# Activation-beacon attention and a soft MoE on one core: first loads, beacon requests, a weight piece and the next pair's first score bank are moved

## The chip, the cores and the metric

The kernel runs on one core of a Trainium2 chip. The metric is device time in microseconds: before the change 202.38 us, the median of three runs (201.41 to 203.35). The profile is of one further execution.

## The reference

Inputs are float32: q, k, v of 8 batches x 8 heads x 576 tokens x 64, beacon_k and beacon_v of 16 positions per head, phi (512 x 32), and eight experts' w1 (512 x 1024) and w2 (1024 x 512).

```python
k_all, v_all = concat([beacon_k, k], 2), concat([beacon_v, v], 2)
scores = q @ k_all.T / sqrt(64)           # causal among tokens, beacons always seen
a = softmax(scores); x = (a @ v_all)      # -> 4608 tokens x 512
logits = x @ phi                          # 32 slots, 4 for each of 8 experts
slot_in = softmax(logits, over tokens).T @ x
slot_out[e] = relu(slot_in[e] @ w1[e]) @ w2[e]
out = softmax(logits, over slots) @ slot_out
```

So all tokens have to pass attention before any expert can work, and all experts before any output row exists.

## The kernel before

**Work.** Two heads make a pair; there are 32 pairs n, four (g = 0 to 3) in each of 8 batches b. A pair's transposed scores (keys on partitions) go through four PSUM banks; ScalarE exponentiates each bank to float16 (`scores`, L522), POOL zeroes the masked triangle (`select`, L508), TensorE multiplies by v with a column of ones (`attend`), VectorE divides (`normalize`, three instructions, the last one L552), and TensorE turns x for the logits (`x_transposes`). For each half batch, q and k are turned by TensorE and copied out by VectorE (`transposes`, L486 and L498); half m's turning of k comes in one pair and that of q in the next. `logits` makes the slot scores of a batch and exponentiates them into dT, repeated four times; `dispatch` sums x by slot over the batch; `combine_T` turns dT into eT for the output. In the loop these are done a batch or two late, between pairs.

**v.** It is loaded as vstag, four consecutive tokens on a partition, with the 16 beacons on partitions 0 to 3; `cast_v` makes float16 of it on POOL, and `perm_v` puts the rows in order with 16 selecting products into four accumulators, which ScalarE and VectorE copy to vh. The last 80 tokens come apart (`load_vr`).

**Order.** Every engine executes in the order in which the code names its instructions; an instruction waits for its data and for the slot of the tile that it writes. Slots: q and k staging four each, vstag two, score accumulators two (two banks each), the attend accumulator one, the small PSUM tiles (tag tr) two, and x, bkf and their like two (tag x). All loads but two of the first are issued by SP; POOL issues the weight pieces of 512 KB in float16, cast from float32 on the way, 32 of them (`load_weights`, L449 and L456), the last of them into staging slots of q, k and v as these come free.

**Start and end.** Before the loop stand the first loads, constants, `fill` (products without a use, which keep TensorE busy), the turning of the beacon keys through bkh, PSUM and bkA to kT, and pairs 0 and 1. After it stand the last pair's rest, the experts (`first` L823, `turn`, `second` L838), the scaling of the slot outputs (L860), and the output in 13 requests (L920).

Of the kernel before, what the change touches and what calls it, by code (L numbers as in the profile page):

```python
# [9 lines left out]
FP = mybir.dt.float32  # L10
# [258 lines left out]
def kernel(  # L269
# [38 lines left out]
    phih = const.tile([P, NDC, NSL], F16, name="phih")  # L308
    bkA = const.tile([P, Nb, B * H], BF, name="bkA")

# [44 lines left out]
    def load_v(b):  # L355

        t = st["v", b] = stv.tile([P, H, 4, D], FP, name="vstag", tag="v", bufs=2)
        st["r", b] = stv.tile([P, H, D], FP, name="vrem", tag="r", bufs=2)
        if b:
            lo = (b * H * S - Nb) * D
            nc.sync.dma_start(
                out=t[:, :, :, :].rearrange("p h t d -> p h (t d)"),
                in_=v.rearrange("b h s d -> (b h s d)")[lo:lo + H * S * D].rearrange(
                    "(h e) -> h e", h=H)[:, 0:4 * P * D].rearrange("h (p e) -> p h e", p=P))
        else:
            for p0, p1 in ((4, 116), (116, 128)):  # L370
                nc.sync.dma_start(
                    out=t[p0:p1, :, :, :].rearrange("p h t d -> p h (t d)"),
                    in_=v[b, :, 4 * p0 - Nb:4 * p1 - Nb, :].rearrange(
                        "h (p t) d -> p h (t d)", t=4))

    def load_vr(b):
        nc.sync.dma_start(out=st["r", b][0:80, :, :],
                          in_=v[b, :, 496:576, :].rearrange("h p d -> p h d"))

    def load_bv(b):  # L380
        nc.sync.dma_start(out=st["v", b][0:4, :, :, :].rearrange("p h t d -> p h (t d)"),
                          in_=beacon_v[b].rearrange("h (p t) d -> p h (t d)", t=4))

    def cast_v(b, c):

        if c == 0:
            st["c", b] = work.tile([P, 4, H, D], F16, name="vc", tag="vc", bufs=1)
        if c < 2:
            for hs in (slice(4 * c, 4 * c + 2), slice(4 * c + 2, 4 * c + 4)):
                nc.gpsimd.tensor_copy(  # L390
                    out=st["c", b][:, :, hs, :].rearrange("p t h d -> p h t d"),
                    in_=st["v", b][:, hs, :, :])
        else:
            nc.gpsimd.tensor_copy(out=vhs[b % 2][0:80, 4, :, 0:D], in_=st["r", b][0:80, :, :])

    def perm_v(b):

        ps = ps_sc.tile([P, 2, 512], FP, name="vps", tag="sc")
        pt = [ps_tr.tile([P, 512], FP, name="vpt", tag="tr") for _ in range(2)]
        outs = [ps[:, 0, :], ps[:, 1, :], pt[0][:, :], pt[1][:, :]]  # L400
        vc = st["c", b]
        for t in range(4):
            for c in range(4):
                nc.tensor.matmul(outs[c], sel[32 * c:32 * c + 32, t, :],  # L404
                                 vc[32 * c:32 * c + 32, t, :, :].rearrange("p h d -> p (h d)"),
                                 start=(t == 0), stop=(t == 3))
        nc.scalar.activation(vhs[b % 2][:, 0:2, :, 0:D],  # L407
                             ps[:, :, :].rearrange("p c (h d) -> p c h d", d=D), AF.Copy)
        for i in range(2):
            nc.vector.tensor_copy(out=vhs[b % 2][:, 2 + i, :, 0:D],  # L410
                                  in_=pt[i][:, :].rearrange("p (h d) -> p h d", d=D))
# [49 lines left out]

    def beacon_keys(m):
        for hh in range(2):
            c0, c1 = (H * (m // 2) + head(2 * m + u, hh) for u in range(2))
            nc.gpsimd.tensor_copy(  # L465
                out=kTs[m % 2][64 * hh:64 * hh + 64, :, 0:Nb],
                in_=bkA[64 * hh:64 * hh + 64, :, c0:c1 + 1:c1 - c0].rearrange("p n u -> p u n"))

    def transposes(m, which):
# [6 lines left out]
        else:  # L476
            if m:
                beacon_keys(m)
            dst = kTs[m % 2][:, :, Nb:Nb + S]
        for j0, j1 in ((0, 5), (5, NJ)):  # L480
            tp = ps_tr.tile([P, j1 - j0, P], BF, name="trps", tag="tr")
            for j in range(j0, j1):
# [92 lines left out]
    def logits(b, t0=0, t1=NDC):  # L575
# [10 lines left out]
        if t1 < NDC:  # L586
            return
        if t0 == 0:
            nc.scalar.activation(dTs[b][:, :, :, :],
                                 lp[:, :, :].unsqueeze(2).broadcast_to([P, NC5, 4, NSL]), AF.Exp)  # L590
        else:
            nc.scalar.activation(dTs[b][:, :, 0, :], lp[:, :, :], AF.Exp)
            nc.vector.tensor_copy(
                out=dTs[b][:, :, 1:4, :],
                in_=dTs[b][:, :, 0:1, :].broadcast_to([P, NC5, 3, NSL]))

# [76 lines left out]
    with tc.manual_schedule(engines={ET.PE, ET.DVE, ET.Activation, ET.Pool, ET.SP}):  # L673
        load_qk(0, 0, first=True)
        bkf = work.tile([P, Nb, D], FP, name="bkf", tag="x")
        nc.sync.dma_start(out=bkf[0:B * H, :, :].rearrange("p n d -> p (n d)"),
                          in_=beacon_k.rearrange("b h n d -> (b h) (n d)"))
        load_v(0)
        load_bv(0)
        load_vr(0)  # L680
        load_qk(0, 1)
        load_v(1)
        load_qk(1, 0)
        load_bv(1)
        load_vr(1)
        load_qk(1, 1)
        phif = work.tile([P, NDC, NSL], FP, name="phif", tag="phif", bufs=1)
# [4 lines left out]
        make_identity(nc, idb)  # L692
        make_identity(nc, idh)
        for t in kTs:
            nc.gpsimd.memset(t[:, :, Nb + S:640], 0.0)
# [6 lines left out]
        nc.gpsimd.memset(xT[:, :, S:640], 0.0)  # L702
        nc.gpsimd.memset(sel[:, :, :], 0.0)


        fill(10, False)
        transposes(0, 0)
        fill(2, False)
        transposes(0, 1)
        bkh = work.tile([P, Nb, D], BF, name="bkh", tag="vc", bufs=1)  # L710
        hi = bkf[0:B * H, :, :].bitcast(BF)[:, :, 1::2]
        nc.scalar.activation(bkh[0:B * H, 8:Nb, :], hi[:, 8:Nb, :], AF.Copy)
        nc.vector.tensor_copy(out=bkh[0:B * H, 0:8, :], in_=hi[:, 0:8, :])
        bkp = ps_tr.tile([P, Nb, B * H], BF, name="bkps", tag="tr")
        for i in range(Nb):
            for hh in range(2):
                nc.tensor.transpose(bkp[64 * hh:64 * hh + 64, i, :], bkh[0:B * H, i, :],
                                    idb[0:B * H, 0:B * H])
        nc.vector.tensor_copy(out=bkA[:, :, :], in_=bkp[:, :, :])  # L719
        beacon_keys(0)  # L720
        fill(5, False)
        for c in range(4):
            for t in range(4):
                nc.vector.tensor_copy(
                    out=sel[32 * c:32 * c + 32, t, :].rearrange(
                        "p (m t) -> p m t", t=4)[:, :, t],
                    in_=idh[32 * c:32 * c + 32, 32 * c:32 * c + 32])


        scores(0, 0, False)  # L730
        scores(0, 1, False)
        for c in range(2):
            cast_v(0, c)
        for bank in range(2):
            fill(3, False)
            scores(0, 2 + bank, False)
        for bank in range(4):
            select(0, bank)
        cast_v(0, 2)
        for bank in range(3):  # L740
            fill(3, False)
            scores(1, bank)
        transposes(1, 0)
        perm_v(0)
        scores(1, 3)
        transposes(1, 1)
        attend(0, 0)
        attend(0, 1)
        normalize(0)
        load_v(2)  # L750
        load_qk(2, 0)

        for n in range(2, NPAIR):
            b, g = divmod(n, NG)
            scores(n, 0)
            scores(n, 1)
            if n // 2 + 1 < 2 * B:
                transposes(n // 2 + 1, n % 2)
            attend(n - 1, 0)
            scores(n, 2)  # L760
            if n >= 3:
                x_transposes(n - 3)
            attend(n - 1, 1)
            if n >= 7 and g == 3:
                combine_T(b - 1)
            normalize(n - 1)
            scores(n, 3)
            if n == NPAIR - 1:
                x_transposes(n - 2)
            if b and g == 2:  # L770
                logits(b - 1)
            if n >= 8 and g == 0:
                dispatch(b - 2)
            if b + 1 < B and g:
                parts = ((0,), (1,), (2,))[g - 1] if b else ((0,), (1, 2))[g - 2]
                for c in parts:
                    cast_v(b + 1, c)
                if g == 3:
                    perm_v(b + 1)
            if b + 2 < B:  # L780
# [3 lines left out]
                if g == 2:  # L784
                    load_bv(b + 2)
                    load_vr(b + 2)
                    load_qk(b + 2, 1)
            if n == 5:
                nc.vector.tensor_copy(out=phih[:, :, :], in_=phif[:, :, :])
            load_weights((0, 1, 1, 1)[g] if b < 6 else 2)  # L790
        siz = work.tile([P, NDC, E * (NSL + SPE)], F16, name="siz", tag="qT")
# [11 lines left out]
        dispatch(B - 2)  # L803
        fill(2)
        x_transposes(n - 1)
# [154 lines left out]
```

## Time and profile before

| what | value |
|---|---|
| median of three runs | 202.38 us |
| profiled execution, its own time | 200.63 us |
| its span, first to last instruction | 198.9 us |
| granted TensorE clock, mean | 0.956 |
| TensorE busy (82%) | 162.4 us |
| ScalarE busy (67%) | 134.0 us |
| VectorE busy (67%) | 132.4 us |
| POOL busy (58%) | 114.8 us |
| moved by DMA | 55.90 MB |
| SP's queue (q1), share of 16 engines' span | 56.0% |
| POOL's queue (q0, weights), the same | 42.3% |
| first exp of pair 0; pair 4; pair 28 | 12.26; 34.66; 137.68 us |
| last weight request issued | 154.4 us |
| first output request | 170.66 us |

The page gives busy time per engine over the whole span, and a row of 40 slices shows where in the span it lies. The DMA row is the mean busy share of 16 engines. The stretches give the same for any window, with the number of instructions in brackets, then the granted clock, the DMA share and the bytes moved per time. Bytes of the weight pieces are counted after the cast, so 214 GB/s in a stretch of weights alone stands for twice that read. In the timeline a bracket gives the idle time of the engine ahead of an instruction and what ended it.

### The profile page before, as it was taken

The numbers are of one execution on the slowest core, as the hardware profiler recorded it, in microseconds if no ns is written. First come the engines' busy times: TensorE is split into PE (matmuls) and PEld (weight loads), VectorE is DVE, ScalarE is ACT, GpSimd is POOL, SyncE is SP. The second block draws the span as 40 slices with busy tenths as digits, with TensorE's granted clock in tenths as the row PEclk, the third lists the DMA queues.
The fourth block names the chain that finished last, engine by engine and source line by source line (L and its number), as shares of the span: only waits on it lengthen the run. The fifth ranks groups of instructions, "written<-read, shape, count | busy, mean of one in ns | idle before, by whom it ended". The sixth has DMA issues, their size and how long they took to land.

```text
span 198.9 us, 7368 instructions
## 1 busy us (share of the span) xinstructions
PE 162.4 (82%) x3122; PEld 107.9 (54%) x3122; DVE 132.4 (67%) x279; ACT 134.0 (67%) x172; POOL 114.8 (58%) x264
## 2 busy tenths in 40 slices
PE   6798893889898898988989898898978999875200
PEld 2443561667586576756757665675856844542000
DVE  0352684678888888888789778788855532898300
ACT  2356694688888889888888788888787140783200
POOL 6049087359659847955965786799776400890000
PEclk9999999699999999999999999999999999997855
DMA  6999999999999999999999999999999995599991
GB/s 203 258 240 367 283 357 326 264 377 316 280 242 379 279 258 326 319 258 292 381 249 270 363 305 269 257 229 211 216 211 214 214 213 95 211 410 415 409 403 69
DMA packets 29845, 55.90 MB, mean 281 GB/s; under 512 B 7244, under 2 KB 15660, under 8 KB 29804
## 3 DMA queue, kind: packets, MB, share of 16 engines
q1 hardware_dynamic: 24764, 37.98, 56.0%
q0 software_dynamic: 4752, 16.78, 42.3%
q10 hardware_dynamic: 288, 0.59, 1.0%
q8 instruction: 26, 0.43, 0.8%
q14 instruction: 15, 0.12, 0.2%
HBM read 62.69 MB, written 9.44 MB: 363 GB/s over the span
## 4 chain that ended last, share of the span: by engine, by line


## 5 line engine op out<-in xcount | busy, mean ns | idle before, releaser
L522 ACT ACTIVATE expT<-sc 128x992 f16<-128x992 f32 (+3 forms) x128 | 104.8, 867 | 20.3 <-PE sc L517 19.7
L508 POOL TENSOR_SCALAR_AFFINE_SELECT expT<-expT 128x224 f16<-128x224 f16 (+3 forms) x128 | 55.1, 441 | 39.6 <-ACT expT L522 38.7
L517 PE MATMUL sc<-qT,kT 64*128 64x80 bf16 (+4 forms) x576 | 43.7, 246 | 11.2 <-ACT expT L522 5.4
L538 PE MATMUL av<-vh,expT 128*128 128x65 f16 (+1 forms) x960 | 40.3, 195 | 0.2 <-DVE x L552 0.2
L538 PEld LDWEIGHTS <-expT 128*128 128x128 f16 (+1 forms) x960 | 33.6, 98 | 4.3 <-POOL expT L508 0.8
L498 DVE COPY kT<-trps 128x640 bf16<-128x640 bf16 (+1 forms) x31 | 22.7, 773 | 19.6 <-PE trps L486 19.1
L517 PEld LDWEIGHTS <-kT 64*128 64x128 bf16 x576 | 17.1, 95 | 28.2 <-issue 22.4
L498 DVE COPY qT<-trps 128x640 bf16<-128x640 bf16 (+1 forms) x30 | 22.0, 773 | 8.4 <-PE trps L486 6.6
L552 DVE TENSOR_TENSOR x<-av,r 128x640 f16<-128x640 f32 x32 | 26.4, 824 | 1.1
L390 POOL CAST vc<-vstag 128x512 f16<-128x512 f32 x32 | 18.7, 614 | 1.6 <-ACT expT L522 1.6
L571 DVE COPY xT<-xtps 128x576 f16<-128x576 f16 x31 | 14.1, 456 | 6.0 <-PE xtps L564 5.8
L914 ACT ACTIVATE osb<-fps,rc 128x512 f32<-128x512 f32 (+1 forms) x18 | 11.2, 675 | 10.2 <-PE fps L909 9.5
L564 PE MATMUL xtps<-idh,x 128*128 128x128 f16 (+2 forms) x160 | 14.3, 217 | 0.4 <-issue 0.2
L916 DVE TENSOR_SCALAR osb<-fps,rc 128x512 f32<-128x512 f32 (+1 forms) x19 | 12.8, 727 | 1.3 <-PE fps L909 1.2
L658 PE MATMUL fill<-eT,onesh 128*128 128x512 f16 x36 | 11.6, 451 | 1.7 <-POOL onesh L691 1.5
L407 ACT ACTIVATE vh<-vps 128x1024 f16<-128x1024 f32 x8 | 8.2, 1027 | 6.6 <-PE vpt L404 6.6
L410 DVE CAST vh<-vpt 128x512 f16<-128x512 f32 x16 | 10.3, 684 | 3.6 <-PE vpt L404 3.6
L564 PEld LDWEIGHTS <-x 128*128 128x128 f16 (+2 forms) x160 | 9.2, 98 | 6.0 <-issue 5.5
L909 PE MATMUL fps<-so,eT 128*128 128x512 f16 (+1 forms) x37 | 11.2, 431 | 1.2 <-DVE so L860 0.8
L465 POOL COPY kT<-bkA 64x32 bf16<-64x32 bf16 x32 | 7.4, 232 | 7.9 <-DVE bkA L719 7.0
L486 PE MATMUL trps<-idb,kstag 128*64 128x128 bf16 x270 | 11.7, 234 | 0.1
L486 PE MATMUL trps<-idb,qstag 128*64 128x128 bf16 x270 | 10.9, 222 | 0.7 <-DVE vh L410 0.4
(98 smaller groups left out, 187.6 us busy)
## 6 DMA issues: line engine op xcount, KB each, us to landing
kstag<-in_k_dram SPq DMA_DIRECT2D x15, 576.0 KB, 10.0
qstag<-in_q_dram SPq DMA_DIRECT2D x15, 576.0 KB, 13.6
out_dram<-osb SPq DMA_DIRECT2D x11, 768.0 KB, 7.2
vstag<-in_v_dram SPq DMA_DIRECT2D x7, 1024.0 KB, 14.8
w1h<-in_moe_w_dram POOLq DMA_DIRECT2D x10, 512.0 KB, 8.6
w2h<-in_moe_w_dram POOLq DMA_DIRECT2D x10, 512.0 KB, 8.4
wt<-in_moe_w_dram POOLq DMA_DIRECT2D x7, 512.0 KB, 12.2
wv<-in_moe_w_dram POOLq DMA_DIRECT2D x4, 512.0 KB, 11.6
```

The costliest lines, as they stand in the source:

```text
L390: nc.gpsimd.tensor_copy(out=st["c", b][:, :, hs, :].rearrange("p t h d -> p h t d"), in_=st["v", b][:, hs, :, :])
L486: nc.tensor.transpose(tp[lo:hi, j - j0, :], t[:, hh, j, :].bitcast(BF)[:, 1::2], idb[:, :])
L498: nc.vector.tensor_copy(out=do, in_=ti)
L508: nc.gpsimd.affine_select(out=ap, in_=ap, compare_op=AL.is_ge, fill=0.0, base=cbase, pattern=pat, channel_multiplier=-1)
L517: nc.tensor.matmul(sc[:, hh, col:col + qw], kTs[n // 2 % 2][po:po + D, n % 2, c * P:(c + 1) * P], qTs[n // 2][po:po + D, n % 2, q0:q0 + qw ...
L522: nc.scalar.activation(ex[:, :, base:base + w], sc[:, :, 0:w], AF.Exp, scale=scale)
L538: nc.tensor.matmul(av[:, i, :], exps[n % 2][0:KW[c], hh, o:o + P], vhs[b % 2][0:KW[c], c, h, :], start=(c == 0), stop=(c == i))
L552: nc.vector.tensor_tensor(out=xs[b][:, :, head(n, 0):head(n, 1) + 1:head(n, 1) - head(n, 0), :].rearrange("p i h d -> p h i d"), in0=av[:, ...
L564: nc.tensor.transpose(tp[:, QLO[i]:QLO[i] + QW[i]], xs[b][0:QW[i], i, 2 * t:2 * t + 2, :].rearrange("p h d -> p (h d)"), idh[0:QW[i], 0:QW ...
L571: nc.vector.tensor_copy(out=xT[:, t, 0:S], in_=tp[:, :])
L658: nc.tensor.matmul(ps[:, :], onesh[:, :], eT[:, 0:512], start=True, stop=True)
L916: nc.vector.tensor_scalar(out=ou, in0=f[:, 0:hw], scalar1=rc[:, bb, j:j + 1], scalar2=None, op0=AL.mult)
```

## The change

Loads. v of batch 0 comes as one request over 128 partitions for heads 1 to 7 and two requests (60 and 64 partitions) for head 0, whose first four partitions POOL zeroes. `load_bv` is gone: beacon_v of batch 0 comes as 16 partitions x 8 heads and that of all batches as one request of 128 partitions. beacon_k comes as 128 partitions x 2 KB in place of 64 x 4 KB. `load_qk(1, 0)` stands ahead of `load_v(1)`.

v. The selecting matrix has zeros for the beacons' rows, and `perm_v` adds them by one product from bvh. For batch 0 it accumulates in the attend banks, and two of its casts are VectorE's; batch 1's casts stand a pair earlier.

Beacon keys. One copy of bkf by VectorE, 16 products of 128 x 128, and kT written from PSUM by VectorE for half 0; bkA is copied after it.

Loop. `scores(n + 1, 0)` stands at the end of pair n; banks 2 and 3 stand ahead of the two halves of `attend`. `combine_T` moves to g = 0 and `dispatch` to g = 1 of the batch after the next, each behind the bank and behind `normalize`. `logits` exponentiates one copy on ScalarE and VectorE repeats it. One weight piece is issued ahead of the loop, one less in batch 5.

```diff
     def load_v(b):
-        if b:
...
-        else:
-            for p0, p1 in ((4, 116), (116, 128)):
...
+        h0 = 0 if b else 1
+        lo = ((b * H + h0) * S - Nb) * D
+        nc.sync.dma_start(
+            out=t[:, h0:H, :, :].rearrange("p h t d -> p h (t d)"),
...
+        if b == 0:
+            nc.gpsimd.memset(t[0:4, 0, :, :], 0.0)
+            for p0, p1 in ((4, 64), (64, 128)):
                 nc.sync.dma_start(
+                    out=t[p0:p1, 0, :, :].rearrange("p t d -> p (t d)"),
+                    in_=v[b, 0, 4 * p0 - Nb:4 * p1 - Nb, :].rearrange("(p t) d -> p (t d)", t=4))
...
-    def load_bv(b):
...
     def cast_v(b, c):
-                nc.gpsimd.tensor_copy(
+                (nc.vector if c == 1 and b == 0 else nc.gpsimd).tensor_copy(
...
     def perm_v(b):
-        ps = ps_sc.tile([P, 2, 512], FP, name="vps", tag="sc")
+        pool, tag = (ps_sc, "sc") if b else (ps_av, "av")
+        ps = pool.tile([P, 2, 512], FP, name="vps", tag=tag)
...
+        rows(0, 0)
+        lhsT, rhs = (idh[:, b::B], bvh) if b else (idh[0:Nb, 0:Nb], bvh[0:Nb])
+        nc.tensor.matmul(outs[0][0:Nb, :], lhsT, rhs[:, :, :].rearrange("p h d -> p (h d)"),
+                         start=False, stop=False)
...
     def logits(b, t0=0, t1=NDC):
-        if t0 == 0:
-            nc.scalar.activation(dTs[b][:, :, :, :],
-                                 lp[:, :, :].unsqueeze(2).broadcast_to([P, NC5, 4, NSL]), AF.Exp)
-        else:
...
+        nc.scalar.activation(dTs[b][:, :, 0, :], lp[:, :, :], AF.Exp)
+        nc.vector.tensor_copy(
+            out=dTs[b][:, :, 1:4, :],
+            in_=dTs[b][:, :, 0:1, :].broadcast_to([P, NC5, 3, NSL]))
...
         load_v(0)
-        load_bv(0)
+        bv0 = work.tile([P, H, D], FP, name="bv0", tag="x")
+        nc.sync.dma_start(out=bv0[0:Nb, :, :], in_=beacon_v[0].rearrange("h n d -> n h d"))
         load_vr(0)
         load_qk(0, 1)
+        load_qk(1, 0)
         load_v(1)
-        load_qk(1, 0)
-        load_bv(1)
         load_vr(1)
+        bvf = work.tile([P, H, D], FP, name="bvf", tag="x")
+        nc.sync.dma_start(out=bvf[:, :, :], in_=beacon_v.rearrange("b h n d -> n b h d"))
         load_qk(1, 1)
...
         transposes(0, 0)
-        fill(2, False)
+        bkh = work.tile([P, Nb // 2, D], BF, name="bkh", tag="vc", bufs=1)
+        nc.vector.tensor_copy(out=bkh[:, :, :], in_=bkf[:, :, :].bitcast(BF)[:, :, 1::2])
         transposes(0, 1)
...
+        beacon_keys(0, bkp[:, :, :].rearrange("p n (c a) -> p n c a", a=2), nc.vector)
+        nc.vector.tensor_copy(out=bkA[:, :, :, :].rearrange("p n c a -> p n (c a)"),
+                              in_=bkp[:, :, :])
+        fill(3)
...
+        scores(1, 0)
+        perm_v(0)
+        scores(1, 1)
         transposes(1, 0)
-        perm_v(0)
+        scores(1, 2)
+        attend(0, 0)
+        transposes(1, 1)
         scores(1, 3)
-        transposes(1, 1)
-        attend(0, 0)
         attend(0, 1)
         normalize(0)
         load_v(2)
         load_qk(2, 0)
+        load_weights(1)
+        scores(2, 0)
         for n in range(2, NPAIR):
             b, g = divmod(n, NG)
-            scores(n, 0)
             scores(n, 1)
             if n // 2 + 1 < 2 * B:
                 transposes(n // 2 + 1, n % 2)
+            scores(n, 2)
             attend(n - 1, 0)
-            scores(n, 2)
             if n >= 3:
                 x_transposes(n - 3)
+            scores(n, 3)
             attend(n - 1, 1)
-            if n >= 7 and g == 3:
-                combine_T(b - 1)
             normalize(n - 1)
-            scores(n, 3)
             if n == NPAIR - 1:
                 x_transposes(n - 2)
+            else:
+                scores(n + 1, 0)
+            if b > 1 and g == 0:
+                combine_T(b - 2)
+            if b > 1 and g == 1:
+                dispatch(b - 2)
             if b and g == 2:
                 logits(b - 1)
-            if n >= 8 and g == 0:
-                dispatch(b - 2)
...
-                    load_bv(b + 2)
                     load_vr(b + 2)
...
-            load_weights((0, 1, 1, 1)[g] if b < 6 else 2)
+            load_weights((0, 1, int(b < 5), 1)[g] if b < 6 else 2)
...
         dispatch(B - 2)
-        fill(2)
+        combine_T(B - 2)
         x_transposes(n - 1)
```

## The prediction

> **What bounds the kernel now.** The page's slices first: is there an engine without gaps?
>
> ```profile
> PE   6798893889898898988989898898978999875200
> ...
> DMA  6999999999999999999999999999999995599991
> ```
>
> No compute engine fills its slices, but the 16 DMA engines stand at 9 from the second slice to the 33rd, and again while the output leaves. A share of 9 doesn't yet say that useful bytes move, so next the stretches (the last two columns are the DMA share and GB/s):
>
> ```profile
> 6.00:8.00 2.00, 1.94 (x22) 1.16 (x24) 0.82 (x1) 0.51 (x1) 0.00 (x0) 1.00 1.05 202
> 8.00:10.00 2.00, 1.04 (x36) 0.87 (x36) 1.15 (x2) 1.43 (x3) 0.00 (x0) 1.00 1.12 262
> 10.00:12.00 2.00, 2.00 (x30) 0.93 (x26) 1.51 (x9) 0.00 (x0) 0.50 (x2) 1.00 1.29 155
> 12.00:14.00 2.00, 1.87 (x14) 0.72 (x11) 1.02 (x10) 1.74 (x3) 0.63 (x2) 1.00 1.13 261
> 14.00:16.00 2.00, 2.00 (x17) 0.70 (x16) 0.00 (x0) 1.64 (x4) 2.00 (x5) 1.00 1.07 389
> ...
> 21.00:22.00 1.00, 0.50 (x12) 0.39 (x11) 1.00 (x3) 1.00 (x2) 0.00 (x0) 1.00 0.81 301
> 22.00:23.00 1.00, 1.00 (x29) 0.90 (x29) 0.74 (x1) 0.79 (x2) 0.33 (x1) 1.00 0.95 181
> ```
>
> From 6 to 14 us the engines are full and yet move half of what they move at 14 to 16. At 21 to 23 they are not even full. Later, 30 to 134, the share is 1.07, and it is 1.06 up to 163: no room. Then the end of the loads:
>
> ```profile
> 164.00:165.00 1.00, 1.00 (x19) 0.36 (x17) 0.46 (x1) 0.35 (x1) 0.00 (x0) 1.00 0.95 182
> 165.00:166.00 1.00, 1.00 (x20) 0.78 (x20) 0.28 (x1) 0.00 (x0) 0.00 (x0) 1.00 0.81 152
> 166.00:167.00 1.00, 1.00 (x28) 0.42 (x20) 0.42 (x1) 0.00 (x0) 0.00 (x0) 1.00 0.74 137
> 167.00:168.00 1.00, 1.00 (x23) 0.35 (x16) 0.00 (x0) 0.00 (x0) 0.00 (x0) 1.00 0.17 31
> ```
>
> The last weight piece, issued at 154.39, lands at 168.14 (the trace's landing of that request). The timeline there shows who needs it:
>
> ```profile
> 168.19 0.39 PE L838 MATMUL so<-w2h,hT 128*32 128x512 f16 x1
> ...
> 168.82 0.75 DVE L860 TENSOR_SCALAR so<-so,rd 128x512 f16<-128x512 f32 x1 [2.40 <-PE so L838]
> ```
>
> TensorE comes to the last four products at 168.19 after idling at most 0.5 us (its weight load's idle time there is 0.51). So two chains end together: the loads at 168.14, TensorE's own at about 167.9. Behind them stands the output, 9.44 MB at 414 GB/s, 22.8 us, which the change doesn't touch. To shorten the span both chains must shorten.
>
> **The loads' chain, part by part.** This is the one that I expect to decide.
>
> (a) The first loads of batch 0's v went out as 112 and 12 partitions and a beacon request of 4. In 6 to 14 us 2 x (202+262+155+261) = 1,760 KB moved; at 371 GB/s (mean of 389, 350 and 374 at 14 to 20) that takes 4.7 us, so 3.3 are lost. Of these 0.5 is the remainder of v, 164 KB in 256-byte rows, which in batch 1 also moves slowly (181 at 22 to 23), and stays. Afterwards seven heads go as 128 partitions, as batch 1's do at 350 to 374; head 0, 124 rows, stays in two odd pieces, 0.3 us if they are as slow as now. Gain 2.5; from 0 (the slowness belongs to the moment, not the shape) to 3.3.
>
> (b) SP waited 39.1 us in the loop to write a beacon over a landed v tile:
>
> ```profile
> SPq L381 <- DMA vstag<-in_v_dram: 39.1, 7, 6.6
> ```
>
> Mostly other loads were queued meanwhile and the share stayed at 1.06. Only the first wait, 6.6 us until 20.79, let the queue run dry: 0.81, 0.95 and 0.98 in 21 to 24 make 0.25 + 0.11 + 0.08 = 0.44 us. Gain 0.4 (0 to 0.44).
>
> (c) From 164 the shares lack 0.11 + 0.25 + 0.32 + 0.89 of 1.06, or 1.5 us: some engines are through, others not; the packets' own times show 17 at once until 164.4, some 13 until 166.6 and 4 at 167.4. Requests of 4 and 12 partitions are what could load the engines unequally, and these go. But the output, all of it in 128 partitions, fades as well (0.56, 0.26, 0.02 after 1.04 in 194 to 197, 1.2 us before 196). Gain 0.6, from 0 to 1.5. The Trainium skill (DMA: Bandwidth & Descriptors, "Why a DMA increments its semaphore by 16 and not by 1") says that a request uses the largest number of engines up to 16 that divides its slowest dimension, so 4 for a beacon request and 12 for the 12 partitions. The fade's steps agree with it; by it alone (c) would be the whole 1.5.
>
> (d) The beacons of v now come as 1,152 rows of 256 bytes, 295 KB, for 256 rows of 1 KB. At the 192 GB/s of 22 to 24 that is 1.5 us, less 262 KB at 371, 0.7: cost 0.8. From 0.4 to 2.6 (the packets of 256 bytes took 19 ns in the loop, 25 at 22 to 24, 49 at 10 to 14: 1,152 x 49 over 17 in flight is 3.3, less 0.7).
>
> The beacon keys as 128 rows of 2 KB instead of 64 of 4 KB, and the piece of weights moved ahead, change no bytes: 0 in a queue that is full anyway. Sum: 2.5 + 0.4 + 0.6 - 0.8 = 2.7 us.
>
> **TensorE's chain must give as much, 2.7 less its slack of about 0.2.**
>
> Start: the keys of the beacons now go from ScalarE's and VectorE's copies (until 9.94) through TensorE, a 0.69 us copy and two POOL copies to the first score at 11.55. Afterwards fill(2), 7.38 to 7.92, is gone; the copy of bkf (0.41 for half, one engine, 128 partitions) stands ahead of qT's 0.82 copy, and two VectorE copies from PSUM (0.23 each in POOL's row, which I take) replace 0.69 + 0.56. First score about 9.7: 1.9 us. The 16 sel copies (1.97) move ahead of everything on VectorE, which idles until 7.06, behind idh at 2.5. The new memsets (head 0's four rows, on POOL ahead of fill's data, some 0.2; sel's rows) are covered by the k load, which lands at about 6.2. The copy to bkA (0.69) now stands behind the score path.
>
> Pairs 0 to 3: the rows to look at are
>
> ```profile
> 32.67 0.39 PE L404 MATMUL vps<-vc,sel 32*128 32x512 f16 x2 [2.38 <-POOL vc L390]
> ...
> 35.00:40.00 5.00, 4.35 (x73) 3.13 (x71) 3.05 (x7) 3.13 (x5) 1.88 (x6) 0.69 1.07 267
> ```
>
> TensorE waits 2.4 us for POOL to cast v of batch 1, and then runs at a granted clock of 0.69. The casts now stand a pair earlier: from pair 3 to 4 the first exps lie 7.43 us apart, and from 7 to 8, with a perm_v too, 4.82: 2.6 us. In pair 1 the exp of bank 3 waited behind perm_v (18.66 to 21.55); with perm_v's accumulators in the idle av banks another 1 to 2. Together 5 to 6 by pair 4, twice what is needed. What is late next there is the loads themselves.
>
> Loop: every pair now shows two waits, TensorE for ScalarE before bank 1 (0.57 at 43.69) and ScalarE for TensorE before bank 2 (0.27 at 45.63). With the next pair's bank 0 written ahead, ScalarE's four exps (3.3 us busy a pair) can run on. But TensorE's own work is 16.8 us a batch (first exps of pairs 8 and 12, 52.71 to 69.51) less these waits, some 15.8; perm_v gets one product more (0.22 in issue), dT goes from ScalarE's 0.70 to 0.30 plus VectorE's 0.31. Gain 0 to 1 us a batch. One wait is added: x has two slots, and dispatch of batch b-2, which reads the one that the first normalize of batch b writes, now stands behind it in the code. VectorE's multiply (0.82) then waits for 25 products (0.93) and bank 0 (0.33); behind it are kT's copies (1.46), and for them TensorE's attend. About 1 us a batch in six batches, mostly under ScalarE's exps.
>
> So TensorE gains 4 us or more and the loads 2.7: the loads decide, and what TensorE gains more becomes waiting for k, q or weights. Span 198.9 - 2.7 = 196.2; with the 1.7 us around it 197.9 for the profiled execution of 200.63. That execution is 1.75 under the median shown, so I take the difference from the median: **199.7 us**.
>
> **Rivals.**
>
> Weights starve the loads: in 53 to 59 both queues were full and the packets in flight were 4 of k, q and v against 13 of weights. If pairs come sooner, weights are issued sooner; three more pieces ahead of the last q (2.45 us each, the spacing of landings after 140) delay it from 134 by 7.35 - 2.7 to 138.7, where pair 28 needs it at 138.1 now. Then TensorE's tail decides, the gain falls to about 1: 201.4. It decides from the third piece on.
>
> The first loads stay slow: what the kernel's start loses would be a matter of time, not shape. Then 0.4 + 0.6 - 0.8: 202.2, no change.
>
> The beacon request is dear: the Trainium skill (the same page, "Specifications") gives 512 bytes as the least for full rate and a read-modify-write below it; the trace agrees in part, with 192 GB/s for such rows at 22 to 24. As a mechanism here: the 256-byte rows at 49 ns, the slowest that the trace has, 2.6 instead of 0.8, a gain of 0.9: 201.5.
>
> Slower: VectorE's new wait on x. If it isn't hidden, each of six batches pays the bank, the products, the multiply, both copies and the attend that needs them, 0.33 + 0.93 + 0.82 + 1.46 + 0.57 = 4.1 us less the 1 us that the loop's order saves, 18 in all; less the 5 of the start and the 0.2 of slack 13. It decides from 0.9 us a batch net, where it has eaten those 5.2. Halfway, at 2 us a batch, 12 - 5 = 7 us are lost: 209. Against it: VectorE is busy 8.4 of 10 us, so it can catch up 1.
>
> **How the numbers follow.** Loads decide: 0.62. Weights starve: 0.13. First loads stay slow: 0.10. Beacon request dear: 0.08. Slower through x: 0.07. About 1% is what a measurement of this kernel can tell from no change: 2 us. Faster by more than that is the forecast, nearly all of it (0.57), and a part of the weights and beacon cases (0.05): 0.62. Within 1%: 0.31. Slower: 0.07. The range: the best of all bounds, 3.3 + 0.4 + 1.5 - 0.4 = 4.8, gives 197.6, and the runs shown scatter by 1: 196.6. At the other end the cases without gain reach 202.2, with half that scatter 202.7; slower lies outside.
>
> **What would show it.** (a) 6 to 14 us over 330 GB/s, with a first score near 9.7. (b) no share under 1 before 160, no beacon wait in SP's list. (c) the last piece landing near 165.4 with a shorter fade. TensorE idle before its last products by some us more than now. Wrong: the last q landing later than 134, a TensorE that never waits at the end, or VectorE idle ahead of its multiply (L552 now) each fourth pair.

## The result and the profile after

The changed kernel takes 204.54 us (median of four runs, 203.60 to 204.83); the kernel before takes 202.32 beside it. The ratio is 1.0133, 95% interval 1.0094 to 1.0173: slower, where 199.7 was forecast, and above the range. The profiled execution took 204.83 us with a span of 203.1, 4.2 more than before. It is the longest of its four, and that of before (200.63) lies 1.75 under its median, so the 4.2 us that are followed here are more than the 2.2 between the medians.

The page's slices, in the order of the prediction:

```profile
PE   6798959998998897989989998998999999884200
...
PEclk9999996999999999999999999999999879997855
DMA  6999999999999999999999999899999994499992
```

TensorE is now at 9 from the 29th to the 34th slice without a break, up to the stretch ahead of the output; before, two of these six stood at 7 and 8. The stretches of the start (last columns: granted clock, DMA share, GB/s):

```profile
6.00:8.00 2.00, 1.91 (x29) 1.57 (x29) 0.97 (x3) 0.55 (x1) 0.00 (x0) 1.00 1.04 353
8.00:10.00 2.00, 0.90 (x25) 0.81 (x25) 1.05 (x3) 0.64 (x2) 0.00 (x0) 1.00 1.20 303
10.00:12.00 2.00, 1.66 (x11) 0.52 (x11) 1.94 (x5) 1.18 (x3) 1.01 (x2) 1.00 1.07 266
12.00:14.00 2.00, 2.00 (x20) 0.67 (x18) 0.63 (x1) 1.81 (x4) 2.00 (x5) 1.00 1.06 395
...
30.00:36.00 6.00, 5.49 (x87) 3.75 (x87) 3.35 (x6) 3.31 (x4) 2.25 (x6) 0.72 1.09 281
```

The first loads did what was hoped: 2,634 KB from 6 to 14 us for 1,760. The end:

```profile
162.00:163.00 1.00, 1.00 (x16) 0.66 (x18) 0.67 (x3) 0.00 (x0) 0.29 (x1) 0.50 1.05 209
163.00:164.00 1.00, 1.00 (x12) 0.33 (x8) 0.00 (x0) 0.00 (x0) 0.00 (x0) 0.50 1.07 213
...
168.00:169.00 1.00, 1.00 (x25) 0.53 (x21) 0.36 (x1) 0.60 (x1) 0.00 (x0) 1.00 0.88 162
169.00:170.00 1.00, 1.00 (x19) 0.57 (x12) 0.10 (x1) 0.00 (x0) 0.00 (x0) 1.00 0.48 86
170.00:171.00 1.00, 1.00 (x20) 0.43 (x18) 0.69 (x1) 0.00 (x0) 0.00 (x0) 1.00 0.18 33
```

TensorE has no idle time there, while the loads fade away from 168 on: TensorE's chain decides, not the loads. Its last product ends at 172.93, and the last weight piece has landed at 171.46, itself 3.3 us later than before. That piece is issued at 157.58, 1.09 us behind the end of the loop's last exp. The distance is 1.09 us in the profile of before and in every other profile of this case, since POOL issues it behind the masking of the last pair. So the end of the loads is no chain of its own: it can't come before the loop is through, and from that issue to the landing it is 11.4 to 15.4 us in these profiles. The scaling of the slot outputs begins at 172.99 us (before 168.82), and from there to the end both kernels need 30.1.

**Where the time went.** First exps of the pairs, and the two ends:

| first exp of pair | before | after | after minus before |
|---|---|---|---|
| 0 | 12.26 | 11.10 | -1.2 |
| 4 | 34.66 | 26.91 | -7.8 |
| 8 | 52.71 | 47.13 | -5.6 |
| 28 | 137.68 | 139.79 | +2.1 |
| last exp's end | 153.30 | 156.49 | +3.2 |
| scaling of slot outputs | 168.82 | 172.99 | +4.2 |

So the start gained 5.6 us by pair 8; the next 20 pairs lost 7.7, the last four 1.1 and the tail 1.0. An undisturbed batch of the loop takes 18.17 us (first exps of pairs 16 and 20, 85.33 and 103.49, which round to 18.16) where it took 16.71 (86.64 to 103.35). Five batches at 1.46 make 7.3 of the 7.7.

In the lines of the changed kernel L502 and L514 are the transposes and VectorE's copies of them, L533 and L538 the scores and their exps, L401 and L417 perm_v and the copies of its small tiles, L659 and L648 the copies of combine_T and dispatch. What TensorE waits for in the loop, from 46 to 150 us, before (total, times, longest):

```profile
PE sc L517 <- ACT vh L407: 3.9, 6, 0.8
PE sc L517 <- ACT expT L522: 3.3, 6, 0.6
```

and after:

```profile
PE trps L502 <- DVE vh L417: 2.5, 5, 0.5
PE trps L502 <- DVE eT L659: 1.7, 5, 0.3
...
PE trps L502 <- DVE acc L648: 1.2, 4, 0.3
```

The waits for ScalarE are gone, as the change intends. In their place the transposes of q and k wait, for the copies with which VectorE empties the small PSUM tiles of perm_v, combine_T and dispatch. The timeline at the worst place, pair 24, whose bank 0 was written before perm_v:

```profile
121.55 0.39 PE L401 MATMUL vps<-vc,sel 32*128 32x512 f16 x1
...
123.17 0.37 PE L533 MATMUL sc<-qT,kT 64*128 64x384 bf16 x4
...
123.31 1.29 DVE L417 CAST vh<-vpt 128x512 f16<-128x512 f32 x2 [0.74 <-PE vpt L401]
124.05 1.01 PE L502 MATMUL trps<-idb,kstag 128*64 128x128 bf16 x18 [0.51 <-DVE vh L417]
124.19 0.94 ACT L538 ACTIVATE expT<-sc 128x928 f16<-128x928 f32 x1
...
125.00 0.34 PE L533 MATMUL sc<-qT,kT 64*128 64x128 bf16 x4
...
125.44 0.81 ACT L538 ACTIVATE expT<-sc 128x768 f16<-128x768 f32 x1 [0.31 <-PE sc L533]
```

perm_v holds both small tiles; the transposes can't begin before VectorE's first copy, and their second half not before the second, so 18 products take 1.01 us, where they take 0.69 when both tiles are free. ScalarE, with one bank ahead, still runs dry before bank 2. In the kernel before, the transposes behind a perm_v find both tiles free:

```profile
103.51 0.38 PE L517 MATMUL sc<-qT,kT 64*128 64x384 bf16 x4 [0.61 <-ACT vh L407]
103.81 0.69 PE L486 MATMUL trps<-idb,kstag 128*64 128x128 bf16 x18
```

The listed waits are in total no longer after the change than before. Most of the price stands inside TensorE's groups, where a transpose waits between two products and the page counts the engine as busy. Counted from the start of one group to the start of the next, in the two undisturbed batches above, the transposes of q and k take 4.09 us of a batch for 2.53, x_transposes 1.41 for 1.08 and perm_v 1.62 for 1.32, while the scores fall from 5.76 to 5.18 and attend from 4.38 to 4.20: together the 1.45.

### The profile page after: what moved, and what is told of

The parts are those of the page before. It is cut to its first block, busy times and chain, and to the rows that moved or that the text cites. A ratio compares the mean times of both kernels' runs of the same rounds, so it can differ in the third digit from the quotient of the medians.

```text
span 203.1 us, 7337 instructions
## 1 busy us (share of the span) xinstructions
PE 167.2 (82%) x3099; PEld 109.9 (54%) x3099; DVE 138.2 (68%) x292; ACT 133.9 (66%) x171; POOL 117.1 (58%) x262
## 4 chain that ended last, share of the span: by engine, by line
## 5 line engine op out<-in xcount | busy, mean ns | idle before, releaser
L538 ACT ACTIVATE expT<-sc 128x992 f16<-128x992 f32 (+3 forms) x128 | 108.0, 864 | 22.1 <-PE sc L533 20.4
L533 PE MATMUL sc<-qT,kT 64*128 64x80 bf16 (+4 forms) x576 | 45.3, 246 | 1.4 <-ACT expT L538 0.8
L554 PE MATMUL av<-vh,expT 128*128 128x65 f16 (+1 forms) x960 | 41.2, 195 | 1.6 <-issue 1.6
L533 PEld LDWEIGHTS <-kT 64*128 64x128 bf16 x576 | 17.0, 95 | 15.6 <-issue 6.8
L514 DVE COPY kT<-trps 128x640 bf16<-128x640 bf16 (+1 forms) x31 | 22.7, 773 | 1.3 <-PE trps L502 1.2
L514 DVE COPY qT<-trps 128x640 bf16<-128x640 bf16 (+1 forms) x30 | 21.9, 767 | 0.3 <-PE trps L502 0.3
L386 POOL CAST vc<-vstag 128x512 f16<-128x512 f32 x30 | 17.7, 618 | 6.5 <-DMA vstag<-in_v_dram 6.5
L502 PE MATMUL trps<-idb,kstag 128*64 128x128 bf16 x270 | 13.7, 234 | 5.8 <-DVE vh L417 3.5
L417 DVE CAST vh<-vpt 128x512 f16<-128x512 f32 x16 | 10.3, 688 | 9.0 <-PE vpt L401 9.0
L502 PEld LDWEIGHTS <-kstag 128*64 128x64 bf16 x270 | 10.3, 116 | 10.5 <-issue 10.5
L502 PE MATMUL trps<-idb,qstag 128*64 128x128 bf16 x270 | 13.1, 226 | 3.2 <-DVE eT L659 1.7
L565 DVE TENSOR_SCALAR stat<-av 128x10 f32<-128x10 f32 x32 | 5.4, 169 | 13.1 <-PE av L554 13.1
L580 PE MATMUL xtps<-idh,x 128*128 128x128 f16 (+2 forms) x160 | 13.7, 216 | 0.2 <-DVE acc L648 0.2
L502 PEld LDWEIGHTS <-qstag 128*64 128x64 bf16 x270 | 9.3, 112 | 7.1 <-issue 7.1
```

Of the source, the lines that this page charges most:

```text
L386: (nc.vector if c == 1 and b == 0 else nc.gpsimd).tensor_copy(out=st["c", b][:, :, hs, :].rearrange("p t h d -> p h t d"), in_=st["v", b][ ...
L502: nc.tensor.transpose(tp[lo:hi, j - j0, :], t[:, hh, j, :].bitcast(BF)[:, 1::2], idb[:, :])
L514: nc.vector.tensor_copy(out=do, in_=ti)
L533: nc.tensor.matmul(sc[:, hh, col:col + qw], kTs[n // 2 % 2][po:po + D, n % 2, c * P:(c + 1) * P], qTs[n // 2][po:po + D, n % 2, q0:q0 + qw ...
L538: nc.scalar.activation(ex[:, :, base:base + w], sc[:, :, 0:w], AF.Exp, scale=scale)
L554: nc.tensor.matmul(av[:, i, :], exps[n % 2][0:KW[c], hh, o:o + P], vhs[b % 2][0:KW[c], c, h, :], start=(c == 0), stop=(c == i))
```

## The experiments

Each time is the median beside the kernel before on the same chip; ratios are to that kernel.

**Only the loop's order undone** (old_loop) and **only the order made** (new_loop_only).

```diff
# old_loop, against the changed kernel
-        scores(2, 0)                     # and in the loop: scores(n + 1, 0)
+            scores(n, 0)                 # at the head of its own pair
+            attend(n - 1, 0); scores(n, 2); ...; attend(n - 1, 1); combine_T; normalize; scores(n, 3)
# new_loop_only: the reverse, against the kernel before
```

Both runs also move combine_T, dispatch and the fill of the tail with the order.

> The changed kernel with the loop's order of before (bank 0 at the head of its own pair, banks 2 and 3 behind the halves of attend, combine_T and dispatch where they were, the fill in the tail); the start, the loads, the beacons and perm_v stay changed. Theory A (the loop's new order costs what was lost, whichever part of it): pairs 8 to 31 take about 97 us again instead of 106, some 4 to 5 us of the start's gain stay until the loads end the chain, so 196 to 199 us. Theory C (the added work decides: one product more in perm_v, VectorE's copies of dT and bvh): pairs 8 to 31 stay near 106 us and the time at 203 to 205.

> The kernel before with only the loop's new order (bank ahead, banks 2 and 3 ahead of the halves of attend, combine_T and dispatch behind the bank, combine_T for the fill in the tail). Theory A: pairs 8 to 31 rise from 97 to about 105 us and nothing of the start is gained: 207 to 212 us. Theory C: within 1 us of before, 201.5 to 203.5.

old_loop: 202.27 us, ratio 0.9977 (0.9922 to 1.0033), no change. new_loop_only: 205.04, ratio 1.0124 (1.0031 to 1.0216). The order alone makes the kernel as slow as the whole change, though it ends 2 us short of the 207 expected. Its batches take 17.88 us, every one from pair 8 on, for 16.71: 1.17 of the 1.46. In those batches the transposes take 1.96 us more than before and x_transposes 0.33, the scores 0.76 less. From pair 8 to 28 it loses 4.4 us, where the changed kernel loses 7.7. Of the 1.46 a batch the rest, 0.29, comes with the added work; perm_v's products alone last from 101.20 to 102.52 before and from 121.55 to 123.17 after, 0.30 more. The first expectation of old_loop failed: without the new order the start's gain doesn't reach the end. Its loop needs 101.2 us from pair 8 to 31 for 97.1, and its last weights land at 169.9, after 168.14 before. That is a second cause, taken up below.

**Which part of the order.** First two parts of it taken back in the changed kernel:

```diff
# extras_first
-                scores(n + 1, 0)          # ahead of the pair's extras
+            scores(n + 1, 0)              # behind them
# attend_first
-            scores(n, 2); attend(n - 1, 0); ...; scores(n, 3); attend(n - 1, 1); normalize(n - 1)
+            attend(n - 1, 0); scores(n, 2); ...; attend(n - 1, 1); normalize(n - 1); scores(n, 3)
```

> The changed kernel with one line moved: the next pair's bank 0 stands behind the extras of the pair (combine_T, dispatch, logits, casts, perm_v) and not ahead of them; banks 2 and 3 stay ahead of the halves of attend. Theory A1 (the extras directly ahead of bank 1 and of the transposes cost it, as the transposes then find both small PSUM tiles still held by the extras' copies on VectorE): pairs 8 to 31 come down to 98 to 101 us, the time to 197 to 200. Theory A2 (banks 2 and 3 ahead of attend cost it): no change, 203.5 to 205.

> The changed kernel with banks 2 and 3 behind the first and second half of attend again, bank 3 behind normalize; the bank ahead and the extras behind it stay. Theory A1 (the extras ahead of bank 1 and the transposes): no gain, 203.5 to 206, with the transposes' waits for VectorE's copies unchanged at 6 us or more. Theory A2 (the order of banks and attend): pairs 8 to 31 at 98 to 101 us, the time 197 to 200.

205.81 us (ratio 1.0179, 1.0087 to 1.0271) and 206.82 (1.0203, 1.0098 to 1.0308): neither brings the loop back. Undisturbed batches take 17.7 to 18.2 and 18.67. Both one-place theories fell, so the three parts were made one by one in the kernel before, one execution each:

```diff
# bank_ahead_only        + scores(n + 1, 0) right behind scores(n, 3)
# banks_first_only       + scores(n, 2) and scores(n, 3) ahead of the halves of attend
# extras_moved_only      + combine_T, dispatch at the end of the first, second pair of batch b + 2
```

> The kernel before with one part of the loop's new order: the next pair's bank 0 stands right behind bank 3, ahead of logits, dispatch and perm_v; banks 2 and 3, combine_T and dispatch stay where they were. An undisturbed batch takes 16.7 us in the kernel before and 17.9 with the whole new order (new_loop_only). If the bank ahead is what costs: 17.5 to 18.7. If it is the extras' place or banks 2 and 3: 16.5 to 17.0.

> The kernel before with another part alone: banks 2 and 3 stand ahead of the first and the second half of attend. If that is what costs: a batch at 17.3 to 18; if the bank ahead or the extras' place: 16.3 to 16.9.

> The kernel before with the third part alone: combine_T and dispatch each stand at the end of the first and second pair of the batch after the next, right ahead of the next pair's bank 0 (and one combine_T more in the tail). If the extras' new place costs by itself: a batch at 17.3 to 18; if only together with the bank ahead, which puts them right ahead of bank 1 and the transposes: 16.6 to 17.1.

Undisturbed batches: 18.15, 17.33 and 16.8 to 16.9 us, for 16.71; times of 211.04, 205.17 and 202.84. So the bank ahead costs most, 1.44 a batch, banks 2 and 3 cost 0.6, the extras' new place 0.1 to 0.2. They don't add up: all together are 1.17, less than the bank alone. The timeline of bank_ahead_only at perm_v shows the same waits as the changed kernel:

```profile
108.08 0.39 PE L404 MATMUL vps<-vc,sel 32*128 32x512 f16 x2 [0.65 <-ACT expT L522]
...
109.19 1.29 DVE L410 CAST vh<-vpt 128x512 f16<-128x512 f32 x2 [0.54 <-PE vpt L404]
109.94 1.01 PE L486 MATMUL trps<-idb,kstag 128*64 128x128 bf16 x18 [0.51 <-DVE vh L410]
...
111.89 0.81 ACT L522 ACTIVATE expT<-sc 128x768 f16<-128x768 f32 x1 [0.88 <-PE sc L517]
```

perm_v's accumulators share the two slots of the scores, so it must now wait for bank 3's exp (0.65); then the transposes wait for its small tiles (0.51 and the longer 1.01); ScalarE stands 0.88 before bank 2. In the kernel before, banks 0 and 1 lie between perm_v and the transposes. That the small tiles and the slots of the scores are what the order pays for is read from these timelines; no run gave the order more of either.

**The extras behind the transposes.** If only the place of the extras between bank 0 and the transposes counted, it should help to put them behind:

```diff
# extras_late, against the changed kernel: logits, dispatch, combine_T, perm_v of pair n - 1
             transposes(n // 2 + 1, n % 2)
+            extras(*divmod(n - 1, NG))
             scores(n, 2)
```

> The changed kernel with its bank ahead and its order of banks and attend; logits, dispatch, combine_T and perm_v of a pair stand behind the next pair's bank 1 and transposes, ahead of its bank 2, and no longer directly ahead of bank 1 (dispatch at the first pair of a batch, combine_T at the second). Theory A1 (the extras' place between bank 0 and bank 1 costs: transposes wait for the small PSUM tiles): the transposes' waits for VectorE's copies, 3.5 and 1.7 and 1.2 us in the changed kernel, fall under 1 us each, an undisturbed batch from 18.17 to 17.0 to 17.5, the time to 201 to 203. Rival (the extras wait for the transposes' copies instead and TensorE loses as much): a batch at 18 or more, 204 to 207.

210.32 us, ratio 1.0438 (1.0360 to 1.0515), 19.5 us a batch: the rival, and worse. The waits of TensorE in the whole span of extras_late:

```profile
PE lgps L599 <- DVE qT L514: 4.8, 6, 0.8
PE sips L634 <- DVE qT L514: 4.7, 6, 0.8
PE etps L656 <- DVE kT L514: 4.0, 5, 0.8
```

Now the extras wait for the transposes' copies. It isn't the extras' place as such: of two neighbours on the small tiles the second waits for VectorE's copies of the first, here up to 0.8 us where it was 0.5.

**The added work mended.** ScalarE makes the copy of the beacon values, the beacons' product goes behind twelve of perm_v's sixteen, and in the changed order the fill is back in the tail.

```diff
# perm_last: old_loop, and new_order_mended: the changed kernel, both with
-            if n == 3: nc.vector.tensor_copy(out=bvh, in_=bvf)
+            if n == 2: nc.scalar.activation(bvh, bvf, AF.Copy)
+            if t == 3: (the beacons' product)            # in perm_v, was behind the first product
# new_order_mended also
+        fill(2)                                          # behind combine_T(B - 2) in the tail
```

> The run old_loop with two of the added pieces of work placed otherwise: the beacons' product stands behind twelve of the sixteen selecting products, so that these go four at a time from the first, and ScalarE makes the float16 copy of all beacon values in pair 2 where VectorE made it in pair 3. Expected by all: the last pair of a batch 5.57 us down to about 5.3, pair 3 from 7.6 to about 5.5 us. Theory D (the loads decide): time unchanged, 201.5 to 202.8. Theory E (TensorE's loop decides): 0.3 us in each of seven batches and 2 us at the start reach the end: 198 to 200.

> The changed kernel, its new loop order kept, with its other additions mended: copy of the beacon values on ScalarE in pair 2, the beacons' product late in perm_v, and the fill back in the tail behind combine_T. If the order itself costs TensorE its time (transposes behind the extras waiting for small PSUM tiles): a batch falls only from 18.17 to about 17.8 us, pair 8 begins at 44 to 45, the tail has no clock under 1.00 and gives back 1 us: 201 to 203. If the additions were what cost it: a batch at 17.0, 196 to 199.

perm_last: 203.21 us, ratio 1.0072 (1.0026 to 1.0117); the last pair of a batch stayed at 5.6 to 5.7 where it was undisturbed, so the product's place wasn't what lengthens it. Pair 4 began at 29.44 for 31.23 in old_loop, but pair 8 at 50.94 for 48.64, and the loads end at 169.7. new_order_mended: 202.79, ratio 1.0031 (0.9990 to 1.0072), 1% under the changed kernel, with undisturbed batches of 17.9 to 18.2 and a clock of 1.00 from 160 to 169: the order keeps its price. Of the 2.9 us between the two profiles, 1.5 lie from pair 8 to 28, most of it in the batches from pair 8 to 16 (18.41 and 18.69 for 18.98 and 19.22), and 0.9 in the tail. Pair 6 began 3.7 us earlier than in the changed kernel (36.0), pair 8 only 0.3: a pair of 6.83 lies between, in which the transposes wait 2.52 us for half of k.

**The loads.** In old_loop the DMA engines stand full, and yet here are two stretches without weights:

```profile
57.00:58.00 1.00, 0.88 (x26) 0.79 (x27) 0.37 (x1) 1.00 (x2) 1.00 (x3) 1.00 1.11 273
58.00:59.00 1.00, 1.00 (x27) 0.79 (x24) 1.00 (x2) 0.24 (x1) 0.99 (x4) 1.00 1.09 261
```

Such stretches moved about 380 GB/s before. Summed from the packets, a 2304-byte packet of q or k takes 98 to 102 ns from 60 to 120 in the kernel before and 111 to 113 in old_loop. Sorted by half microseconds from 30 to 140, those with q and k, with the last 80 tokens of v (load_vr) and without weights are 6 before, at 115 ns, and 41 in old_loop, at 124. (How few weight packets count as none moves such counts: 3 to 8 before, at 104 to 118 ns, and 38 to 48 in old_loop, at 123 to 134.) By 30 us old_loop had moved 0.52 MB of weights more than the kernel before and otherwise as much, 2.4 us at the weights' 214 GB/s; by 100 the lead was gone. Three runs tried its cause:

```diff
# vr_wide_rows: old_loop, and perm_last_vr_wide: perm_last, both with
-        in_=v[b, :, 496:576, :]            # 640 rows of 256 bytes
+        in_=(80 rows of 2 KB from the head of v[b])
# v_split: perm_last with v in two requests of four heads, each between k and q
```

The two kernels with wide rows leave the values of the last 80 tokens out of the result.

> The changed kernel with the loop's order of before (the run old_loop) and, in addition, the last 80 tokens of v fetched as 80 rows of 2 KB and not as 640 rows of 256 bytes: the same bytes, but the wrong tokens, so that part of the values is left out of the computation. Theory D (in old_loop the loads end late, at 169.9 us, because these short rows move while no weights are in flight, and packets of 2304 bytes beside them then take 122 to 133 ns where they take 97 otherwise): the stretches of 285 to 300 GB/s without weights go, packets of 2304 bytes come back from 111 to about 100 ns, the last weights land by 167, the time is 198.5 to 200. Theory D2 (q and k are slowed by something else, for instance by more of SP's requests being queued at once): packets at 108 ns or more, 201.5 to 202.8 us.

> Both of these together: loop order of before, beacons' product late, copy on ScalarE, and the last 80 tokens of v as 80 rows of 2 KB (the wrong tokens, so part of the values is left out). Theory D with TensorE close behind the loads: 197 to 199 us, at least 1 us under the better of the two alone. Theory D2: as perm_last.

> The run perm_last with v of batches 2 to 7 fetched in two requests of four heads, each between a request for k and one for q. Theory D3 (k and q packets are slow, 110 to 125 ns for 97 to 101, whenever neither v's 1 KB rows nor weights move beside them; in the run old_loop that is so in some 27 us between 30 and 140, in the kernel before in some 7): these stretches shrink to under 10 us, packets of 2304 bytes come back to 103 ns or less between 44 and 120, the last weights land 2 to 4 us sooner than 169.7, the time is 199 to 201. Rival (the stretches are slow for another reason, the splitting changes nothing): landing at 169 to 170.5, 202 to 204 us.

vr_wide_rows: 201.33, ratio 0.9949 (0.9892 to 1.0006), packets at 100 to 107 ns, weights landed at 167.15. Yet its profile still has 23 to 34 such half microseconds, at 108 to 113 ns, without a single 256-byte row of v. perm_last_vr_wide: 200.88, ratio 0.9918 (0.9866 to 0.9969); in its profile, of an execution of 202.44 us, there are 46 at 116. So the rows' size is at most a part of the reason. v_split: 207.60, ratio 1.0293 (1.0180 to 1.0405): v's rows now move beside q and k, and where load_vr's are there too and no weights, the packets take 134 ns; where load_vr's aren't, 97 to 101. The slow time goes with that request, not with q and k being alone. Then the request was moved:

```diff
# vr_early: perm_last, with load_vr two pairs earlier
                     load_v(b + 2)
+                    load_vr(b + 2)
                     load_qk(b + 2, 0)
# no_piece_ahead: vr_early without load_weights(1) ahead of the loop, and without the piece less in batch 5
```

> The run perm_last with the request for the last 80 tokens of v moved by two pairs, from ahead of the second k and q of a batch to right behind the request for v. Theory D (q and k packets are slow while that request is under way and no weights are): the half microseconds between 30 and 140 in which it moves with q or k and without weights or v, 28 in perm_last at 124 ns, change their number with the place, the 2304-byte packets come down from 105 to 110 to 103 or less, the last weights land by 168, 200 to 202 us. If the slow stretches stay with q and k themselves: 203 to 204, landing at 169.5 to 170.

> The run vr_early once more, with more rounds: 200 to 202 us if its first time was no chance, 202.5 to 204 if it was.

> The run vr_early with the weights' order of before: no piece ahead of the loop, and none fewer in batch 5. If the piece ahead starves q and k (the rival of the prediction): TensorE's waits for a k half, 3.8 us in vr_early, go, q, k and v moved by 120 us rise from 26.6 MB to 27 or more, the time falls by 1 to 2 us to 199 to 200.5. If the loads are full either way: the last weights land as late or up to 2.5 us later, 201 to 203.

vr_early: 200.96 us, ratio 0.9945 (0.9902 to 0.9989), and the second time 201.50, ratio 0.9953 (0.9917 to 0.9989). Its profile of 199.05 us has 2.7 us of waits for k and 11 half microseconds of q or k beside that request without weights, at 113 to 118 ns. no_piece_ahead: 200.53, ratio 0.9922 (0.9889 to 0.9955), with 0.4 us of waits for k and one of 1.5 for q. Between 54 and 58, again with hardly any weights, but with no row of that request moving:

```profile
54.00:56.00 2.00, 1.49 (x36) 0.92 (x32) 1.35 (x4) 1.80 (x4) 1.44 (x4) 1.00 1.04 400
56.00:58.00 2.00, 2.00 (x55) 1.62 (x49) 1.97 (x4) 1.69 (x3) 1.99 (x6) 1.00 1.05 397
```

In this profile 3 such half microseconds are left, at 95 ns; the packets take 94 to 103 ns in all mixtures, and the weights land at 167.06. vr_early and no_piece_ahead are under both kernels, 0.5 to 0.8% under the kernel before: the changed start and loads with the loop's old order. What taking the piece back adds can't be told; their intervals overlap.

**Everything together, with extras_late:**

> extras_late and vr_early together, with the copy of the beacon values on ScalarE, the beacons' product late in perm_v and the fill behind combine_T in the tail. If both causes are as said: TensorE's last products at 166 to 168, 199 to 201 us. If the loads stay slow: 202 to 203.

214.91 us, ratio 1.0639 (1.0561 to 1.0716): the extras' waits again, 20.09 us a batch.

## Why the prediction was wrong

**The step that failed** is "Loop: ... With the next pair's bank 0 written ahead, ScalarE's four exps can run on ... Gain 0 to 1 us a batch." It asked which wait goes (TensorE's for ScalarE, and it went) and did not ask what is then next to what on TensorE. The order costs 1.17 us a batch and the added work 0.29, in place of a gain of 0 to 1. The next step, "So TensorE gains 4 us or more and the loads 2.7: the loads decide", fell with it: TensorE's slack of 0.2 us was gone, and its chain ended 4.2 us later. Nor did the loads keep their 2.7: the last piece landed at 171.46, not near 165.4.

**Slots were the thing to read.** The small PSUM tiles were named in the description of the kernel, two of them, used by transposes, x_transposes and every extra. Working down the new order with "who held this slot last, and which VectorE copy frees it" would have shown perm_v, the four products of bank 1 and then the transposes. The price, measured as 0.51 and 0.32 us there, could be estimated from rows of before (the two copies of vh at 0.68 each, one behind the other).

**Point by point.** (a) The first loads: 2.5 forecast, 2.4 measured (874 KB more from 6 to 14 us, at 371 GB/s). (b) SP's wait for the beacon is gone. (c) The fade didn't get shorter: 0.18 + 0.58 + 0.88 = 1.6 us lacking from 168 to 171, for 1.5. The requests of 4 and 12 partitions, to which the Trainium skill's rule (DMA: Bandwidth & Descriptors, "Why a DMA increments its semaphore by 16 and not by 1") would give it, are no longer there; the measurement decides against them as the cause. (d) Not isolated; at 40 us the loads were still some 1.8 us ahead, at the two rates of 214 and 371 GB/s. The lower bound of (d), 0.4, does not come out of its rows: 1,152 x 19 ns over 17 less 0.7 is 0.6, which would move the lower end of the range by 0.2 us and nothing else. What the sum of the loads left out is that a full queue need not keep its rate: the head start was lost between 30 and 120 us in stretches of 260 to 300 GB/s.

Start: the first score came at 10.65, not 9.7, since the second half of q's transposes waited 1.19 us for VectorE's qT copy of the first half, behind the new copy of bkf; the changed kernel turns both halves into one tile of the attend accumulator. Pair 3: the wait for POOL's cast went but for 0.40 us, as said, but the prediction didn't price an instruction of the diff, VectorE's copy of all beacon values, queued behind normalize:

```profile
27.73 1.93 DVE L794 CAST bvh<-bvf 128x512 f16<-128x512 f32 x1
...
29.71 0.38 PE L407 MATMUL vps<-bvh,idh 128*16 128x512 f16 x1 [2.13 <-DVE bvh L794]
```

The old wait of 2.38 us became one of 2.13, with a clock of 0.72 behind it. That it cost little by pair 8 is new_order_mended's reading: the loads are late there in any case, as the prediction had it.

The rivals: slower through VectorE's wait on x had the right sign and the wrong place. That wait exists and is small, 3.0 us in six times:

```profile
L568 DVE TENSOR_TENSOR x<-av,r 128x640 f16<-128x640 f32 x32 | 26.4, 824 | 3.9 <-PE sips L634 3.0
```

Weights starving the loads: its sign, a last q later than 134, didn't show in the changed kernel, where the last packet of q ended at 130.3 for 134.8 before; in old_loop it was 140.1, with 0.8 MB of weights more moved by then, so it isn't excluded there. The beacons' short rows: they moved mixed with those of load_vr from 19 to 23 us, at 33 ns a packet from 20 on, between the 25 and the 49 of the forecast, which makes 1.5 us by its reckoning in place of 0.8; no run tells them apart. In the slow stretches later stood other rows, those of load_vr, and making them 2 KB didn't end these, so the Trainium skill's least size of 512 bytes (same page, "Specifications") doesn't explain them alone.

**Open.** The tail's 1.0 us: the first expert products took 3.05 us for 1.91, at a clock of 0.50. The change replaces a fill there by combine_T, but new_loop_only has the same tail and a clock of 1.00 from 160 to 166. And why q and k packets slow down while load_vr's rows move without weights.

## What to carry to other kernels

Before moving work ahead in an engine's order, list for each slot it uses who held it last and which engine's copy frees it: a wait for one engine turned here into waits of 0.3 to 0.8 us for another. A chain with 0.2 us of slack doesn't let the other chain decide for long, so each must be costed as if it decided. And a queue that shows full is not a promise of bytes: check the rate in each stretch, by what moves side by side.

## What was not expected of the hardware

Packets of 2304 bytes took 95 to 102 ns beside v's 1 KB rows, and 113 to 134 ns in most stretches where the 80-partition request of load_vr moved its 256-byte rows without weights (108 to 116 with rows of 2 KB); the share of the engines was 1.04 to 1.16 in these. With that request moved and the piece of weights taken back, q and k moved alone at 400 GB/s with 94 ns a packet, where it had been 260 to 300.
VectorE's copy of 128x512 from SBUF took 1.93 us while POOL masked and cast beside it without a break. The same copy took 1.22 us in old_loop, again with POOL at work throughout, and 0.42 in attend_first, where POOL began a masking 0.15 us behind its start. What sets the three times is not shown.
